# Two weight loads moved to ScalarE's queue, and two small gate operations moved from VectorE to GpSimd, in a kernel of attention and two feed-forward layers

## The chip, the cores and the metric

The kernel runs on one core of one Trainium2 chip. The metric is the time of one execution on the device in microseconds, as the median of several runs. The engines are TensorE (PE in the profile, its weight loads PEld), VectorE (DVE), ScalarE (ACT), GpSimd (POOL) and SyncE (SP), which here only issues transfers.

## The reference

Attention over 4 batches, 8 heads, 576 positions and 64 features per head, mixed with a read from a memory matrix M, then two feed-forward layers over 2304 tokens of width 512 with an inner width of 2048. All inputs are float32.

```python
a = softmax(causal(q @ k.T / sqrt(D)))            # row sums + 1e-9 in the denominator
local = a @ v
q_p = where(q > 0, q, exp(q) - 1) + 1             # phi
mem_out = (q_p @ M_prev) / (q_p @ z_prev + 1e-6)
g = 1 / (1 + exp(-beta))                          # one number per head
x = g * mem_out + (1 - g) * local                 # -> (2304, 512)
h = x @ w_in;  x = (s * relu(h)**2 + b) @ w_out   # layer 1
h = x @ w_in2; out = (h * tanh(softplus(h))) @ w_out2   # layer 2
```

The weights arrive with 64 bits a number; the kernel converts them to float32 itself.

## The kernel before

**Attention.** A unit is one head of one batch. Its query tiles of 128 rows come in two groups, TA (tiles 0 to 2) and TB (tiles 3 and 4). For batch 0 the two groups are units of their own: first TA of all eight heads, then TB of all eight; these 16 units are called early and multiply in plain float32 with 64 rows. The other 24 units (batches 1 to 3) take both groups. In a unit, phi of the query rows is made by GpSimd (line 500), ScalarE (501) and VectorE (502); VectorE multiplies by z and sums (494, 495), which gives the norm in the tile `nm`. The norm gets its epsilon and the head's gate `igate[:, 0, h]` at line 498, in `norm_gate`, and VectorE's reciprocal at line 506. GpSimd then scales phi by it into the first 64 columns of P's rows (557). The scores' maximum is taken by VectorE (545), the exponential and its row sums `rs` by ScalarE (554). The sums get their epsilon and gate `igate[:, 1, h]` at line 574, in `norm`, and a reciprocal at 576; P's rows are multiplied by the result on GpSimd, VectorE or ScalarE (569, 571), by tile. TensorE transposes P (598), multiplies with M and v (626), and the result goes through `xs` (634) to `x_d` in device memory (640).

**Weights.** Each of the 32 pieces of layer 1 (128 rows, 512 numbers of 64 bits) is loaded by SyncE (693) into a `raw` buffer and converted by ScalarE (700, 705, 717) and VectorE (707, 709, 711, 720). The first two raw buffers are the two first thirds of the tile `stage`; four more lie in tiles of later weights.

**Layers.** Layer 1 (products at lines 803 and 877) takes blocks of 256 tokens, later 512. It loads x from `x_d` (820) once all heads of the block's rows are stored, and runs interleaved with the later units. Layer 2 (1009, 1075) follows.

**Order.** Every step is given to a planner with an engine, an expected duration in microseconds, a priority, and the buffers it reads and writes. `Plan.order` simulates the engines and takes on each free engine the ready step with the lowest priority number; the order in which steps start there is the program order on each engine, and each engine works strictly in that order. A change of a duration or of an engine therefore gives another order of the whole program. `NONE` is a pseudo engine for steps that issue nothing. The planner also fills TensorE's planned idle time between 7 and 165 us with products of zeros (`zero_product`, line 1245).

Of the kernel before, what the change touches and what calls it, by code (L numbers as in the profile page):

```python
# [9 lines left out]
F32 = mybir.dt.float32  # L10
F32R = mybir.dt.float32r
BF16 = mybir.dt.bfloat16
I32 = mybir.dt.int32
# [3 lines left out]
ALU = mybir.AluOpType  # L17
AXIS = mybir.AxisListType.X
PSUM = bass.MemoryType.PSUM
DRAM = bass.MemoryType.DRAM  # L20

P = 128
MASKED = -1.0e30
HUGE = 3.0e38
PE, ACT, DVE, POOL, DMA = range(5)
# [25 lines left out]
def act_us(n, extra=0):  # L51
    return 0.094 + 0.00083 * n + 0.093 * extra


def dve_us(n, fast=False):
    return 0.068 + (0.00052 if fast else 0.00104) * n


def pool_us(n):
    return 0.38 + 0.0028 * n  # L60
# [6 lines left out]
def on(letter):  # L67
    return {"A": ACT, "D": DVE, "P": POOL}[letter]
# [111 lines left out]
class Plan:  # L180
# [29 lines left out]
    def add(self, engine, us, prio, f, r=(), w=(), after=(), keep=(), share=1.0):  # L210


        bufs = list({id(b): b for b in (*r, *w, *keep) if b.ring is not None}.values())
        new = [b for b in bufs if b.maker is None]
        waits = {id(s): s for b in r for s in b.writers}
        waits.update((id(s), s) for s in after)
        s = Step(engine, us, prio, f, list(waits.values()), bufs, new)
        s.share = share
        s.left = len(waits)
        for x in waits.values():  # L220
            x.next.append(s)
        for b in bufs:
            b.users += 1
            if b.maker is None:
                b.maker = s
            elif id(b.maker) not in waits:
                b.maker.next_start.append(s)
                s.left += 1
        for b in w:
            b.writers.append(s)  # L230
        self.steps.append(s)
        return s
# [100 lines left out]
def attention_then_two_ffn(ctx: ExitStack, tc: tile.TileContext, qk, qz, vm, beta,  # L333
# [3 lines left out]
    nc = tc.nc  # L337
# [22 lines left out]
    NONE = 5  # L360
    plan = Plan()
    add = plan.add
# [12 lines left out]
    igate = const.tile([P, 2, H], F32, name="igate")  # L375
# [9 lines left out]
    y_in = {j: Buf() for j in range(NT // N1)}  # L385
    wi_in, wo_in, wi_split = ({} for _ in range(3))

    nc.scalar.dma_start(igate[:, 1], beta.partition_broadcast(P))
    nc.scalar.preload_act_table_set("natural_log_exp_and_others")
    nc.scalar.dma_start(sb[:, 0:1], s1.partition_broadcast(P))  # L390
    nc.scalar.dma_start(sb[:, 1:2], b1.partition_broadcast(P))
# [4 lines left out]
    nc.vector.tensor_scalar_add(igate, igate, 1.0)  # L396
    nc.scalar.copy(zeros, mask[:, :P])

    psum = ctx.enter_context(tc.tile_pool(name="psum", bufs=1, space=PSUM))
    banks = [Bank(psum.tile([P, 512], F32, name=f"bank{i}")) for i in range(8)]  # L400
    stage = Home(ctx.enter_context(tc.tile_pool(name="stage", bufs=1, side="right")), "stage", 3072)
    m1 = ctx.enter_context(tc.tile_pool(name="m1", bufs=1))
    small, att = ExitStack(), ExitStack()
    m1s = small.enter_context(tc.tile_pool(name="m1s", bufs=1))
# [28 lines left out]
    def unit(b, h, prio, groups=(TA, TB), place=None):  # L433
# [4 lines left out]
        def add(engine, us, f, r=(), w=(), keep=(), share=1.0, lag=0.0):  # L438
            attention_steps.append(plan.add(engine, us, prio, f, r, w, keep=keep, share=share))
            attention_steps[-1].lag = lag  # L440
# [45 lines left out]
        nm = Buf(R["nm"], [P, 16])  # L486
        lo_t, n_t = tiles[0], len(tiles)
        mine = slice(lo_t, lo_t + n_t)
# [6 lines left out]
            nc.vector.tensor_reduce(nm.t[:, mine], q_rows(), axis=AXIS, op=ALU.add)  # L495

        def norm_gate():
            nc.vector.tensor_scalar(nm.t[:, mine], nm.t[:, mine], 1e-6, igate[:, 0, h:h + 1], op0=ALU.add, op1=ALU.mult)

        add(POOL, 0.4 + 0.0022 * n_t * D, lambda: nc.gpsimd.tensor_scalar_min(ex.t[:, mine], q_rows(), 0.0), [qn_b], [ex])  # L500
        add(ACT, act_us(n_t * D), lambda: nc.scalar.activation(ex.t[:, mine], ex.t[:, mine], AF.Exp), [ex], [ex])
        add(DVE, dve_us(n_t * D), lambda: nc.vector.scalar_tensor_tensor(ex.t[:, mine], q_rows(), 0.0, ex.t[:, mine],
                                                                         op0=ALU.max, op1=ALU.add), [ex, qn_b], [ex])
        add(DVE, 2 * dve_us(n_t * D), norm_phi, [ex, qn_b], [nm, qn_b])
        add(DVE, 0.13, norm_gate, [nm], [nm])
        add(DVE, 0.09, lambda: nc.vector.reciprocal(nm.t[:, mine], nm.t[:, mine]), [nm], [nm])  # L506


# [52 lines left out]
        def norm(tiles):  # L561

            def sums():
                return rs.t[:, tiles[0]:tiles[-1] + 1]

            def scale(t, e):
                x, r = Pt[t].t[:, D:P * (t + 1)], rs.t[:, t:t + 1]
                if e == ACT:
                    nc.scalar.activation(x, x, AF.Copy, scale=r)
                else:  # L570
                    (nc.vector if e == DVE else nc.gpsimd).tensor_scalar(x, x, r, None, op0=ALU.mult)  # L571

            gated, done = Buf(), Buf()
            add(DVE, 0.13, lambda: nc.vector.tensor_scalar(sums(), sums(), 1e-9, igate[:, 1, h:h + 1], op0=ALU.add, op1=ALU.mult),
                [rs_in[t] for t in tiles], [gated], [rs])
            add(DVE, 0.09, lambda: nc.vector.reciprocal(sums(), sums()), [gated], [done], [rs])  # L576
            for t in tiles:
                e = on((E_NORM if early else F_NORM)[t])
                n = D + P * t
                us = act_us(n, 1) if e == ACT else 0.08 + dve_us(n, True) if e == DVE else pool_us(n)  # L580
                add(e, us, lambda t=t, e=e: scale(t, e), [done, Pt[t]], [Pt[t]], [rs])
# [84 lines left out]
    def w_at(nm, r, j):  # L666
        return W[nm, r].t[:, j]
# [8 lines left out]
    def convert(layer, prio, which, r, j, raw, after=()):  # L676


        w_in, w_out = ((w_in1, w_out1), (w_in2, w_out2))[layer - 1]
        fc = r * FPR + j  # L680
        src = w_in[j * P:(j + 1) * P, r * 512:(r + 1) * 512] if which == "in" else w_out[fc * P:(fc + 1) * P, :]
        w = Buf(R["w32"], [P, 512], I32)

        def words():
            return raw.t[:, :1024].rearrange("p (n two) -> p n two", two=2)

        def limbs():
            return raw.t[:, :1024].bitcast(U16).rearrange("p (n four) -> p n four", four=4)

        def f32():  # L690
            return w.t.bitcast(F32)

        add(DMA, 1.5, prio, lambda: nc.sync.dma_start(words(), src.bitcast(I32).rearrange("p (n two) -> p n two", two=2)),
            w=[raw], after=after).lag = 1.4 if layer == 1 else 3.0

        e = on((C_W if layer == 1 else C2_W)[j])
        add(e, 0.567 if e == ACT else 0.335, prio,
            (lambda: nc.scalar.activation(f32(), words()[:, :, 1].bitcast(F32), AF.Copy, scale=2.0 ** -112)) if e == ACT else  # L700
            (lambda: nc.vector.tensor_scalar(f32(), words()[:, :, 1].bitcast(F32), 2.0 ** -112, None, op0=ALU.mult)),
            [raw], [w])

        low_words = Buf()
        add(ACT, 0.567, prio, lambda: nc.scalar.activation(words()[:, :, 0], words()[:, :, 0].bitcast(U32), AF.Copy,
                                                          scale=2.0 ** -29), [raw], [low_words])
        add(DVE, 0.335, prio, lambda: nc.vector.tensor_scalar(w.t, w.t, 3, None, op0=ALU.logical_shift_left), [w], [w])
        signed = Buf()
        add(DVE, 0.542, prio, lambda: nc.vector.tensor_scalar(limbs()[:, :, 1], limbs()[:, :, 3], 0x8000, None, op0=ALU.bitwise_and),
            [raw, low_words], [signed])  # L710
        add(DVE, 0.605, prio, lambda: nc.vector.tensor_tensor(w.t, w.t, words()[:, :, 0], op=ALU.add), [raw, signed, w], [w])  # L711
        if layer == 1:
            hi, lo = f"w{which[0]}h", f"w{which[0]}l"
            hi_dve, lo_dve = C_HI[j] == "D", C_LO[j] == "D"
            half = Buf()
            add(DVE if hi_dve else ACT, 0.335 if hi_dve else 0.52, prio,
                lambda: (nc.vector.tensor_copy if hi_dve else nc.scalar.copy)(w_at(hi, r, j), f32()), [w],
                [W[hi, r], half])
            add(DVE if lo_dve else POOL, 0.6 if lo_dve else 1.23, prio,
                lambda: (nc.vector if lo_dve else nc.gpsimd).tensor_tensor(w_at(lo, r, j), f32(),  # L720
                                                                           w_at(hi, r, j).bitcast(F32), op=ALU.subtract),
                [w, half], [W[lo, r]])
        return w
# [18 lines left out]
    def sums(prio, out, table):  # L742
        for f in table:
            def one(f=f):
                o_, x, y, op = f()
                nc.vector.tensor_tensor(o_, x, y, op=op)

            add(DVE, dve_us(256), prio, one, out[1:], out[:1])
# [383 lines left out]
    for h in range(H):  # L1132
        unit(0, h, PRE_A + STEP_A * h, (TA,), PLACE_A[h % 4])
    for h in range(H):
        unit(0, h, PRE_B + STEP_B * h, (TB,), PLACE_B[h])
# [21 lines left out]
    for i in range(len(seq) + LAG1):  # L1157
        if i < len(seq):
            j, fc = seq[i]
# [4 lines left out]
            n = len(plan.steps)  # L1164
# [4 lines left out]
        if i >= LAG1:  # L1169
            j, fc = seq[i - LAG1]  # L1170
            n = len(plan.steps)
# [3 lines left out]
            if fc == NFC - 1:  # L1175
                n = len(plan.steps)
# [17 lines left out]
    n = len(plan.steps)  # L1194
# [25 lines left out]
    n = len(plan.steps)  # L1220
# [72 lines left out]
```

## Time and profile before

| | |
|---|---|
| median of 3 runs | 1020.19 us (1019.63 to 1021.12) |
| time of the profiled execution | 1016.28 us |
| its span | 1014.3 us |
| TensorE busy | 997.1 us, 98% |
| VectorE busy | 840.7 us, 83% |
| ScalarE busy | 716.1 us, 71% |
| GpSimd busy | 207.8 us, 20% |

The span runs from the first to the last instruction of one profiled execution; its own time includes what lies around it. TensorE's busy time includes the zero products. A busy share is a mean over stages that differ.

### The profile page before, as it was taken

The page shows a single profiled execution, that of the slowest core. Times are in us where ns is not written, and L with a number is a line of the kernel's source. Part 1 is how long each engine was busy: PE and PEld are TensorE (multiplying, and loading weights), DVE is VectorE, ACT ScalarE, POOL GpSimd, SP SyncE. Part 2 cuts the span into 40 slices and gives each one's busy share as a digit, 9 for nine tenths or more (in the row PEclk, how much of TensorE's full clock was granted, in tenths as well). Part 3 has the DMA queues.
Part 4 walks back from the last instruction along what each step waited for, and adds up shares of the span by engine and source line. Part 5 has one row for each costly group of instructions (what it writes and reads, how often), then busy time and mean ns, then how long its engine had stood idle before and what let it go on. Part 6 is the DMA issues. An engine that isn't in the chain of part 4 may idle for free.

```text
span 1014.3 us, 19945 instructions
## 1 busy us (share of the span) xinstructions
PE 997.1 (98%) x6754; PEld 927.5 (91%) x6754; DVE 840.7 (83%) x2163; ACT 716.1 (71%) x1606; POOL 207.8 (20%) x330
## 2 busy tenths in 40 slices
PE   6999999999999999999999999999999999999998
PEld 4658799999999999999888888899999999999998
DVE  7989999999999999986788885279975789567864
ACT  6988798788888788876879997456653466434552
POOL 7841133334344334320000000000010000000010
PEclk9999999999999999999999999999999999999999
DMA  9764553324423433307889986468687665766464
GB/s 272 209 176 143 163 178 99 112 83 122 129 83 101 119 94 99 102 21 216 265 273 311 300 288 216 146 224 270 208 299 258 217 221 176 262 223 219 145 224 171
DMA packets 88981, 188.60 MB, mean 186 GB/s; under 512 B 8752, under 2 KB 63024, under 8 KB 81584
## 3 DMA queue, kind: packets, MB, share of 16 engines
q1 hardware_dynamic: 81392, 135.95, 43.1%
q0 software_dynamic: 7056, 51.38, 15.0%
q8 instruction: 53, 0.87, 0.3%
q14 instruction: 48, 0.39, 0.1%
q10 hardware_dynamic: 432, 0.01, 0.0%
HBM read 144.32 MB, written 42.99 MB: 185 GB/s over the span
## 4 chain that ended last, share of the span: by engine, by line
PE 69%; issue 18%; DVE 6%; POOL 3%; DMA 3%; ACT 1%; SPq 0%; POOLq 0%; DVEq 0%; ACTq 0%
PE bank L877 19%; PE bank L803 19%; PE bank L1009 9%; PE bank L1075 6%; PE bank L626 6%; PE bank L598 4%; PE bank L540 2%; PE bank L541 2%; PE bank L536 1%; POOL Pt L571 1%; DMA woh<-wi_split_d 1%; DVE stage L711 1%; DVE Pt L545 1%; POOL wol L990 1%; DMA stage<-in_w_in 1%
## 5 line engine op out<-in xcount | busy, mean ns | idle before, releaser
L1075 PE MATMUL bank<-woh,S 128*128 128x256 f32 x792 | 107.2, 283 | 0.0
L1075 PEld LDWEIGHTS bank<-woh,S 128*128 128x128 f32 x792 | 100.8, 192 | 0.0
L1075 PE MATMUL bank<-wol,S 128*128 128x256 f32 x720 | 98.1, 283 | 0.0
L557 POOL TENSOR_SCALAR Pt<-ex,nm 128x64 f32<-128x64 f32 x148 | 73.5, 513 | 112.8 <-DVE nm L506 48.9
L1009 PE MATMUL bank<-wi,woh 128*128 128x384 f32 x426 | 94.1, 335 | 0.1
L1075 PEld LDWEIGHTS bank<-wol,S 128*128 128x128 f32 x720 | 91.8, 192 | 0.0
L554 ACT ACTIVATE Pt<-Pt,mx 128x64 f32<-128x64 f32 (+4 forms) x148 | 81.6, 553 | 12.2 <-DVE mx L545 11.9
L990 POOL DMA_DIRECT2D wol<-wo_split_d x17 | 9.2, 540 | 353.6 <-DVE wi L732 261.8
L1009 PEld LDWEIGHTS bank<-wi,woh 128*128 128x128 f32 x426 | 75.6, 188 | 0.8 <-DMA woh<-wi_split_d 0.3
L1009 PE MATMUL bank<-wi,wol 128*128 128x384 f32 x294 | 76.1, 334 | 0.0
L598 PE MATMUL bank<-ident,Pt 128*128 128x128 f32 x432 | 65.6, 278 | 3.8 <-POOL Pt L571 3.6
L571 POOL TENSOR_SCALAR Pt<-Pt,rs 128x64 f32<-128x64 f32 (+2 forms) x68 | 54.4, 832 | 61.1 <-DVE rs L576 47.9
L606 DVE TENSOR_TENSOR PTl<-bank,PTh 128x128 fp32r<-128x128 f32 (+1 forms) x144 | 64.2, 481 | 1.4 <-ACT PTh L603 0.8
L545 DVE CUSTOM_DVE_ANT_0 Pt<-bank,mask 128x320 f32<-128x320 f32 (+3 forms) x148 | 59.7, 416 | 2.0 <-PE bank L541 1.0
L598 PEld LDWEIGHTS bank<-ident,Pt 128*128 128x128 f32 x432 | 49.1, 141 | 10.7 <-POOL Pt L571 7.5
L603 ACT CAST PTh<-bank 128x128 fp32r<-128x128 f32 (+1 forms) x144 | 55.3, 432 | 2.4 <-PE bank L598 1.2
L877 PE MATMUL bank<-gl,woh 128*128 128x256 f32 x320 | 53.7, 290 | 0.0
L877 PE MATMUL bank<-gh,wol 128*128 128x256 f32 x320 | 53.3, 289 | 0.0
L1009 PEld LDWEIGHTS bank<-wi,wol 128*128 128x128 f32 x294 | 53.0, 188 | 0.2
L877 PE MATMUL bank<-gh,woh 128*128 128x256 f32 x320 | 52.2, 285 | 0.0
L803 PE MATMUL bank<-xh,wi 128*128 128x256 f32 x320 | 51.4, 287 | 0.6 <-DVE rt L854 0.4
L848 ACT ACTIVATE rt<-bank,sb 128x256 f32<-128x256 f32 x80 | 38.0, 475 | 17.6 <-PE bank L803 16.1
(280 smaller groups left out, 2900.7 us busy)
## 6 DMA issues: line engine op xcount, KB each, us to landing
wol<-wo_split_d POOLq DMA_DIRECT2D x17, 1024.0 KB, 5.3
woh<-wo_split_d POOLq DMA_DIRECT2D x16, 1024.0 KB, 5.4
qk<-in_qk SPq DMA_DIRECT2D x24, 608.0 KB, 3.9
stage<-in_w_out SPq DMA_DIRECT2D x23, 512.0 KB, 4.2
wo_split_d<-high SPq DMA_DIRECT2D x44, 256.0 KB, 3.8
stage<-in_w_in SPq DMA_DIRECT2D x21, 512.0 KB, 5.0
stage<-wi_d SPq DMA_DIRECT2D x24, 384.0 KB, 4.6
wi_split_d<-woh SPq DMA_DIRECT2D x8, 1024.0 KB, 4.8
```

Source lines behind the costliest of these rows:

```text
L545: nc.vector.tensor_tensor_reduce(Pt[t].t[:, D + lo:D + hi], ps.t[:, :hi - lo], mask[:, SP - w + lo:SP - w + hi], -SCALE, mx.t[:, t:t + 1] ...
L554: nc.scalar.activation(Pt[t].t[:, D:w + D], Pt[t].t[:, D:w + D], AF.Exp, bias=mx.t[:, t + i:t + i + 1], scale=-1.0, accum_out=rs.t[:, t:t ...
L557: add(POOL, 0.48, lambda: nc.gpsimd.tensor_scalar(Pt[t].t[:, :D], ex.t[:, t, :], nm.t[:, t:t + 1], 1.0, op0=ALU.mult, op1=ALU.mult), [ex, ...
L571: (nc.vector if e == DVE else nc.gpsimd).tensor_scalar(x, x, r, None, op0=ALU.mult)
L598: nc.tensor.transpose(ps.t[:, c - c0, :], Pt[t].t[:, c * P:(c + 1) * P], ident)
L603: (nc.vector.tensor_copy if dve else nc.scalar.copy)(PT[0].t[:, at_], ps.t[:, :n])
L606: nc.vector.tensor_tensor(PT[1].t[:, at_], ps.t[:, :n], PT[0].t[:, at_].bitcast(F32), op=ALU.subtract)
L626: nc.tensor.matmul(o.rearrange("p (t q) -> p t q", q=P), v, x.t[:, f[0]:f[-1] + 1:f[1] - f[0] if len(f) > 1 else 1, :], start=(c == 0 and ...
L803: nc.tensor.matmul(ph, w_at(nm, r, cc)[:, o:o + P], x_at(x, cc), start=(part == 0 and cc == 0), stop=(part == 2 and cc == NCC - 1))
L877: nc.tensor.matmul(acc[ec // per].t[:, (ec % per) * n:(ec % per + 1) * n], w_at(nm, r, jj)[:, ec * P:(ec + 1) * P], t(x), start=(big and f ...
L1009: nc.tensor.matmul(ps.t[:, :H2], w[i // 4].t[:, j, kk, i % 4], x[kk].t[:, k], start=begin and part == kk == 0, stop=part == 2 and kk == 1, ...
L1075: nc.tensor.matmul(acc[t].t[:, :DH], s.t[:, j, t * P:(t + 1) * P], x.t[:, k, q % 4], start=q == part == 0, stop=q == NQ2 - 1 and part == 2)
```

## The change

The two parts of the change are independent in the code. The loads of the first two pieces of w_in are issued from ScalarE's queue right behind the load of beta, before the plan; in the plan they are steps of the pseudo engine that are said to be ready after 5.5 and a further 1.0 us. The PSUM pool, the banks and the stage tile are made earlier in the code for that. And lines 498 and 574 are issued on GpSimd, with a planned duration of 0.39 us in place of 0.13.

```diff
@@ -385,7 +385,14 @@
+    psum = ctx.enter_context(tc.tile_pool(name="psum", bufs=1, space=PSUM))
+    banks = [Bank(psum.tile([P, 512], F32, name=f"bank{i}")) for i in range(8)]
+    stage = Home(ctx.enter_context(tc.tile_pool(name="stage", bufs=1, side="right")), "stage", 3072)
+
     nc.scalar.dma_start(igate[:, 1], beta.partition_broadcast(P))
+    for j in range(2):
+        nc.scalar.dma_start(stage.tile([P, 1024], I32, 1024 * j, "raw").rearrange("p (n two) -> p n two", two=2),
+                            w_in1[j * P:(j + 1) * P, :512].bitcast(I32).rearrange("p (n two) -> p n two", two=2))
     nc.scalar.preload_act_table_set("natural_log_exp_and_others")
...
-    psum = ctx.enter_context(tc.tile_pool(name="psum", bufs=1, space=PSUM))
-    banks = [Bank(psum.tile([P, 512], F32, name=f"bank{i}")) for i in range(8)]
-    stage = Home(ctx.enter_context(tc.tile_pool(name="stage", bufs=1, side="right")), "stage", 3072)
@@ -495,14 +499,14 @@
         def norm_gate():
-            nc.vector.tensor_scalar(nm.t[:, mine], nm.t[:, mine], 1e-6, igate[:, 0, h:h + 1], op0=ALU.add, op1=ALU.mult)
+            nc.gpsimd.tensor_scalar(nm.t[:, mine], nm.t[:, mine], 1e-6, igate[:, 0, h:h + 1], op0=ALU.add, op1=ALU.mult)
...
-        add(DVE, 0.13, norm_gate, [nm], [nm])
+        add(POOL, 0.39, norm_gate, [nm], [nm])
@@ -571,7 +575,7 @@
-            add(DVE, 0.13, lambda: nc.vector.tensor_scalar(sums(), sums(), 1e-9, igate[:, 1, h:h + 1], op0=ALU.add, op1=ALU.mult),
+            add(POOL, 0.39, lambda: nc.gpsimd.tensor_scalar(sums(), sums(), 1e-9, igate[:, 1, h:h + 1], op0=ALU.add, op1=ALU.mult),
                 [rs_in[t] for t in tiles], [gated], [rs])
@@ -690,8 +694,11 @@
-        add(DMA, 1.5, prio, lambda: nc.sync.dma_start(words(), src.bitcast(I32).rearrange("p (n two) -> p n two", two=2)),
-            w=[raw], after=after).lag = 1.4 if layer == 1 else 3.0
+        if layer == 1 and which == "in" and r == 0 and j < 2:
+            add(NONE, (5.5, 1.0)[j], prio, lambda: None, w=[raw])
+        else:
+            add(DMA, 1.5, prio, lambda: nc.sync.dma_start(words(), src.bitcast(I32).rearrange("p (n two) -> p n two", two=2)),
+                w=[raw], after=after).lag = 1.4 if layer == 1 else 3.0
```

## Rows read from the trace of the kernel before

**Rows 1.** Busy time by stage: us; PE, PEld, DVE, ACT, POOL busy (instructions); clock; DMA share; GB/s.

```profile
0.00:74.01 74.01, 62.61 (x309) 41.81 (x309) 62.89 (x205) 59.76 (x162) 52.16 (x73) 1.00 0.77 223
74.01:140.00 65.99, 65.99 (x435) 54.60 (x436) 61.91 (x184) 56.58 (x129) 12.79 (x23) 1.00 0.51 154
140.00:170.00 30.00, 28.48 (x229) 27.23 (x228) 29.76 (x80) 24.71 (x59) 10.03 (x13) 1.00 0.41 128
170.00:460.00 290.00, 289.21 (x2334) 283.90 (x2334) 274.18 (x882) 240.99 (x641) 106.69 (x174) 1.00 0.33 96
460.00:1014.30 554.30, 550.75 (x3454) 519.97 (x3453) 411.99 (x816) 334.07 (x619) 26.09 (x49) 1.00 0.71 235
```

**Rows 2.** The same for line 1245, the zero products (PE and PEld busy).

```profile
0.00:74.01 74.01, 21.52 (x119) 17.17 (x119) 1.00 0.77 223
74.01:140.00 65.99, 1.19 (x6) 0.81 (x6) 1.00 0.51 154
140.00:170.00 30.00, 6.30 (x36) 5.12 (x36) 1.00 0.41 128
```

**Rows 3.** Chain of waits up to 170 us: start, us, what.

```profile
2.51 5.44 DMA stage<-in_w_in
56.58 1.04 POOL Pt L571
66.56 5.40 DMA xr<-x_d
74.29 0.47 PE bank L803 x4
```

**Rows 4.** Busy time by stage again, the stretch of the eight heads.

```profile
8.71:60.65 51.94, 47.45 (x245) 32.54 (x244) 48.91 (x161) 46.09 (x130) 47.93 (x59) 1.00 0.83 244
```

**Rows 5.** Timeline, ScalarE and VectorE at the first piece: start, duration, engine; idle before.

```profile
7.97 0.66 ACT L700 ACTIVATE stage<-stage 128x512 f32<-128x512 f32 x1 [2.80 <-DMA stage<-in_w_in]
...
8.67 0.43 DVE L707 TENSOR_SCALAR stage<-stage 128x512 int32<-128x512 int32 x1 [1.99 <-ACT stage L700]
```

**Rows 6.** VectorE's time by stage in line 498 (first three) and 574.

```profile
8.71:60.65 51.94, 2.77 (x8) 1.00 0.83 244
60.65:170.00 109.35, 2.22 (x10) 1.00 0.49 150
170.00:460.00 290.00, 5.28 (x21) 1.00 0.33 96
...
8.71:60.65 51.94, 1.82 (x8) 1.00 0.83 244
60.65:170.00 109.35, 2.90 (x12) 1.00 0.49 150
170.00:460.00 290.00, 10.14 (x44) 1.00 0.33 96
```

**Rows 7.** GpSimd's groups by form, 3.7 to 60.65 us: busy us, mean ns.

```profile
L557 POOL TENSOR_SCALAR Pt<-ex,nm 128x64 f32<-128x64 f32 x22 | 14.0, 657 | 1.4 <-DVE nm L506 0.7 <-DVE mx L545 0.6
L500 POOL TENSOR_SCALAR ex<-qn 128x128 f32<-128x128 f32 x1 | 1.6, 1551 | 0.0
L500 POOL TENSOR_SCALAR ex<-qn 128x192 f32<-128x192 f32 x2 | 1.4, 692 | 0.2
L500 POOL TENSOR_SCALAR ex<-wih 128x128 f32<-128x128 f32 x1 | 0.5, 527 | 0.0
```

**Rows 8.** Line 557 alone, 7 to 64 us: shortest, median, longest ns.

```profile
L557 POOL TENSOR_SCALAR Pt<-ex,nm x22: 309/422/2508, 10.2 to 60.3; 128x64 f32<-128x64 f32 x22
```

**Rows 9.** Timeline of VectorE around a gate.

```profile
66.80 0.22 DVE L574 TENSOR_SCALAR rs<-rs,igate 128x2 f32<-128x2 f32 x1
66.93 0.74 DVE L709 TENSOR_SCALAR wih<-wih 128x512 uint16<-128x512 uint16 x1
```

**Rows 10.** A conversion instruction of VectorE, 8.71 to 60.65 us: busy us, mean ns.

```profile
L709 DVE TENSOR_SCALAR stage<-stage 128x512 uint16<-128x512 uint16 x6 | 4.6, 763 | 0.0
```

**Rows 11.** GpSimd's waits, 170 to 460 us: total us, times, longest.

```profile
POOL ex L500 <- DMA qn<-in_qz: 33.6, 13, 4.1
```

## The prediction

> **What bounds the kernel now.** I read the profile by stages first: the span cut where the work changes, with the busy time of each engine in each piece [rows 1], and beside it how much of TensorE's time in those pieces is its filler, the products of a tile of zeros that keep it occupied and compute nothing [rows 2]. The reader is to see that TensorE does nothing useful for 74.01 - 62.61 + 21.52 = 32.9 us before layer 1 starts at 74, for 1.2 us from 74 to 140, for 30.00 - 28.48 + 6.30 = 7.8 us from 140 to 170, for 0.8 us from 170 to 460, and for 3.6 us after that. That is 46.3 us out of 1014.3, and everything else is products that the change leaves alone. So the end can move only by the moment at which layer 1 begins, and by the 9.0 us lost between 74 and 170. All pieces show the granted clock at 1.00, so the clock has no part in it.
>
> Then the chain that ended last, up to 170 us [rows 3]. Layer 1's first product at 74.29 waits for the load of x at 66.56 (5.40 us), which waits for the last of the eight heads of the first unit group; that head was released by a multiplication on GpSimd at line 571. The chain starts with a weight piece whose load takes 5.44 us from 2.51. In the stretch in which the eight heads run, from 8.71 to 60.65, no engine has room: VectorE is busy 48.91 us of 51.94, GpSimd 47.93, ScalarE 46.09 [rows 4]. From 140 to 170 VectorE is busy 29.76 of 30.00 while TensorE wastes its 7.8 us: there VectorE sets the pace [rows 1, 2].
>
> **The change part by part.**
>
> *The first two pieces from ScalarE's queue.* ScalarE waits 2.80 us for the first piece and starts on it at 7.97; behind it VectorE idles 1.99 us [rows 5]. Its load is the fourth that SyncE issues, at 2.51. ScalarE's queue can issue it right behind the load of beta, about 1.3 us earlier, and with the same 5.44 us it lands 1.3 us earlier. That is the gain's end: -1.3 us. The other end: the two pieces are 1 MB, the chip moved 244 GB/s in the stretch that follows [rows 4], so they take 4.3 us, and q and k of the first head, issued by SyncE meanwhile, could land up to 4.3 us later. SyncE loses two issues and so issues the other heads' loads a little earlier; ScalarE issues two more before its table load, in a time when it has nothing else. I take -0.5 us: a short idle stretch on VectorE is partly filled, and part of it is given back by the first head's loads.
>
> [...] The rows show one queue's loads landing some 5 us after their issue, and nothing of two queues side by side. [...]
>
> *Gates on GpSimd, first stage.* 16 gates lie between 8.71 and 60.65 (8 at line 498, 8 at line 574), 22 between there and 170, and 65 from 170 to 460 [rows 6]. GpSimd has no instruction of 2 to 5 elements a row. The nearest is line 557, 64 elements with the same two scalar operands: 309 ns at its shortest, 422 in the median, 657 as the mean of 22 in this stretch [rows 7, 8]. Below it the price is bounded by line 500: 527 ns at 128 elements and 692 at 192 [rows 7] make 2.6 ns an element and leave 0.20 us for none. So a gate costs between 0.20 and 0.66 us, 3.2 to 10.5 us for 16. I take 0.40, nearest to the median with fewer elements: 6.4 us. Against it stand GpSimd's idle 4.0 us in the stretch [rows 4], of which I count half, and 2.1 us of later units' work at line 500 (128 elements, 527 and 1551 ns) [rows 7] that can move behind the heads: +2.3 us on layer 1's start. The bounds: if all 4.0 us are usable nothing is left on GpSimd, and VectorE's relief, 2.1 us below, brings the heads forward, -2.1; if no idle time is usable and each gate costs 0.66, it is 10.5 - 2.1 = +8.4. Each gate also adds two hand-overs (VectorE or ScalarE to GpSimd, GpSimd to VectorE) to each head's chain; two heads are in flight, so I put them within these bounds. Behind a gate on GpSimd stand lines 557 and 571, for which the transposes on TensorE wait; behind the reciprocal on VectorE stand conversions and the next head's scores.
>
> *VectorE's relief.* The gates' own time is 4.6 us before 60.65 and 5.1 us from there to 170 [rows 6], but VectorE overlaps small instructions: a gate starts at 66.80 and the next instruction at 66.93 [rows 9]. What leaves VectorE is thus nearer 0.13 us a gate: 2.1 us in the first stretch, which goes to conversions that have to be done by 170 anyway, and 2.9 us after it, 5.0 in sum. Between 74 and 170 TensorE wastes 9.0 us and VectorE is the bound where most of it is lost, so I take -4.0 us; the bounds are 0 (nothing reaches TensorE) and -9.0 (all of the waste, with the gates at their full time).
>
> *From 170 to 460.* TensorE wastes 0.8 us there [rows 1]; the 65 gates can give back at most that: -0.5 us, cover being TensorE itself, which is full. VectorE has 290.00 - 274.18 = 15.8 us to spare, and 65 x 0.13 = 8.5 more. If that cover were gone, each wait of VectorE for GpSimd would count in full; that is the third rival.
>
> **Sum.** -0.5 + 2.3 - 4.0 - 0.5 = -2.7 us. The profiled execution's span is 1014.3 us and its own time 1016.28; by the sum they become 1011.6 and 1013.6. The median before is 1020.19, 3.9 above the profiled execution, so the time I give is 1020.2 - 2.7 = 1017.5.
>
> **The rivals.**
>
> *GpSimd becomes the pace of the heads (slower).* For it: GpSimd is busy 92% of the first stage, and one and the same instruction takes 309 to 2508 ns there [rows 8], so it is held by something. Against it: 4.0 us idle and work that can move. With gates at 0.66 us and no idle time used, layer 1 starts 8.4 us later; with -4.0 and -0.5 given back and nothing from the pieces the sum is +3.9: 1024.1. It decides as soon as layer 1's start moves by over 5 us, that is, from 16 x c - 4.1 = 5, a gate at 0.57 us. If each gate has to sit out one whole conversion instruction of VectorE, 763 ns in the mean of line 709 [rows 10], on top of 309 ns, it costs 1.07 us; layer 1 then starts 16 x 1.07 - 4.1 = 13 us later, and the time is 13 - 4.5 = 8.5 above, 1028.7. The spread of line 557 allows it; its median of 422 ns speaks against every gate paying it. [...]
>
> *The two sides cancel (no change).* The start moves by +2.3 and VectorE's relief is spent on waits for the gates, so that only 2 us of the 9.0 come back: 1020.2 within a microsecond. For it: each relieved VectorE instruction is replaced by a wait for another engine. Against it: the order on each engine is planned anew, with the gate's own cost, so other work is put between.
>
> *VectorE waits behind GpSimd in the long stage (slower).* From 170 on GpSimd stands idle at line 500 for q, 33.6 us over 13 waits [rows 11]. A gate that is queued behind such a wait holds the reciprocal, and VectorE with it. VectorE's room is 15.8 + 8.5 = 24.3 us, 0.37 us for each of 65 gates; at 0.5 us each the loss is 8 us: 1028. Against it: line 502 on VectorE already depends on GpSimd and ScalarE, and GpSimd is only 37% busy there.
>
> **How the numbers follow.** This measurement tells a change from none at about 0.2%, 2 us. Forecast (faster, 1011 to 1018): 0.47. Cancelling, within 2 us either way: 0.26. GpSimd the pace: 0.18; every gate behind a whole VectorE instruction: 0.03. Waits in the long stage: 0.04; first head's loads late by most of 4.3 us: 0.02. So faster 0.47, same 0.26, slower 0.27. The forecast's own range is 1012 to 1018.1; to leave out no more than 2 in 10 the range goes from 1011 (the pieces at -1.3, the start unmoved, -8 of the waste) to 1025 (the first rival and a little).
>
> **What would show it.** Right: the first conversion on ScalarE starts near 6.7 us instead of 7.97; gates on GpSimd last 0.2 to 0.66 us; layer 1's first product lies at 74 to 78; the zero products after 140 shrink from 6.30 us to under 3. Wrong: layer 1 starts after 79; GpSimd is busy over 97% up to then and lines 557 and 571 follow each other without a gap; VectorE shows idle time at the two reciprocals; the first scores on TensorE start after the first piece's conversion. The sum would also be wrong if the new order alone, with no price behind it, puts a conversion before a head's work: then the start moves with GpSimd not full.

## The result and the profile after

The changed kernel takes 1026.95 us (median of 7 runs, 1022.64 to 1030.21) against 1019.63 us for the kernel before on the same chip (7 runs): ratio 1.0066, 95% interval 1.0045 to 1.0086. It is slower; the forecast was 1017.5 and its range ended at 1025. The profiled execution has a span of 1021.1 us and a time of 1022.83.

Busy time by stage of the changed kernel (columns as in [rows 1]; the last window runs past the end of the span at 1021.1), and then the zero products, now at line 1252 (as in [rows 2]):

```profile
0.00:74.01 74.01, 56.51 (x260) 38.12 (x260) 56.76 (x168) 53.36 (x143) 57.04 (x87) 1.00 0.71 201
74.01:140.00 65.99, 64.92 (x408) 51.03 (x408) 57.47 (x164) 55.44 (x127) 17.74 (x38) 1.00 0.53 161
140.00:170.00 30.00, 29.48 (x227) 27.66 (x226) 29.46 (x81) 26.72 (x68) 10.97 (x18) 1.00 0.53 159
170.00:460.00 290.00, 288.97 (x2354) 285.58 (x2355) 270.92 (x831) 243.86 (x651) 132.05 (x244) 1.00 0.33 97
460.00:1100.00 640.00, 555.61 (x3490) 524.53 (x3488) 413.70 (x820) 335.82 (x622) 26.09 (x49) 1.00 0.62 203
```

```profile
0.00:74.01 74.01, 22.02 (x112) 17.32 (x112) 1.00 0.71 201
74.01:140.00 65.99, 2.17 (x14) 1.79 (x14) 1.00 0.53 161
140.00:170.00 30.00, 0.96 (x4) 0.68 (x4) 1.00 0.53 159
170.00:460.00 290.00, 1.53 (x9) 1.20 (x9) 1.00 0.33 97
```

The time without useful products before 74 grows from 32.9 to 74.01 - 56.51 + 22.02 = 39.5 us. From 74 to 140 it grows from 1.2 to 3.2, and from 140 to 170 it falls from 7.8 to 30.00 - 29.48 + 0.96 = 1.5. After that it grows again, from 0.8 to 290.00 - 288.97 + 1.53 = 2.6 up to 460 and from 3.6 to 1021.10 - 460.00 - 555.61 = 5.5 from there to the end. In sum TensorE loses 6.0 us more, of the 6.8 by which the span grows. VectorE does 6.1 us less work in the first stage and 3.3 less from 170 to 460 [rows 1]; GpSimd does 4.9 and 25.4 more. So the loss is at the start, most of it comes back by 170, and 3.7 us are lost after 170. In the timeline layer 1's first product moves from 74.13 us to

```profile
87.55 1.70 PE L810 MATMUL bank<-xh,wi 128*128 128x256 f32 x12
```

which is 13.4 us, while the span grows by 6.8. I read that as follows: conversions and later units that stand between layer 1's first products in the kernel before are done by then in the changed one. The window from 140 to 170 agrees (7.8 to 1.5 us); no run tests it alone.

In the timeline of SyncE the first and the eighth head's result go to device memory at these times, first in the kernel before and then in the changed one (start, duration):

```profile
20.64 0.50 SPq L640 DMA_DIRECT2D x_d<-xs  x1
...
65.33 0.55 SPq L640 DMA_DIRECT2D x_d<-xs  x1
```

```profile
29.51 0.55 SPq L644 DMA_DIRECT2D x_d<-xs  x1
...
76.77 0.55 SPq L644 DMA_DIRECT2D x_d<-xs  x1
```

The first head is 8.9 us late already, the eighth 11.4. Two things have to be explained: what happens before 29 us, and what keeps the heads from making it up.

The first half stands in ScalarE's timeline. The kernel before made the gate's exponential and then the first head's at

```profile
4.50 0.22 ACT L395 ACTIVATE igate<-igate 128x16 f32<-128x16 f32 x1 [2.05 <-DVE igate L394]
...
4.81 0.36 ACT L501 ACTIVATE ex<-ex 128x192 f32<-128x192 f32 x1
```

and the changed kernel at

```profile
1.17 0.94 ACTq L394 DMA_DIRECT2D stage<-in_w_in  x2
2.14 1.28 ACT L396 ACT_TABLE_LOAD   x1 [2.14 <-issue]
8.48 0.33 ACTq L397 DMA_DIRECT2D sb<-in_s  x1
9.72 0.33 ACTq L398 DMA_DIRECT2D sb<-in_b  x1
10.11 0.21 ACT L402 ACTIVATE igate<-igate 128x16 f32<-128x16 f32 x1 [6.68 <-DMA wih<-in_vm]
...
10.41 0.66 ACT L707 ACTIVATE stage<-stage 128x512 f32<-128x512 f32 x1
...
10.97 0.35 ACT L505 ACTIVATE ex<-ex 128x192 f32<-128x192 f32 x1
```

The reader is to see the hole between 3.42 and 8.48. The pieces are issued at 1.17 as forecast. The first piece is there when it was forecast: it lands 5.6 us after its issue, near 6.8. But the loads of s and b (512 bytes each), which stood right behind beta, now stand behind the pieces, and each waits: s is issued when the first head's q and k have landed (8.48), b when its v has (9.72), and SyncE issued both of these. Four loads of SyncE wait in the same way: two that start at 6.75 and 9.40 for the two pieces (1.5 and 2.1 us), two that start at 10.34 and 11.76 for loads of the second head (0.6 and 1.1). The trace shows these waits; what ties each load to the one it waits for was not shown. All of ScalarE's arithmetic stands behind the two loads of 512 bytes in the program, and the first of it starts at 10.11, where the kernel before had it at 4.50.

The first head's loads also land later beside the pieces. Loads by group, first 6.5 us (KB, median us to landing), first of the kernel before and then of the changed one:

```profile
wih<-in_qk SPq DMA_DIRECT2D x1, 192.0 KB, 5.1
...
wih<-in_vm SPq DMA_DIRECT2D x1, 96.0 KB, 4.8
```

```profile
wih<-in_qk SPq DMA_DIRECT2D x1, 192.0 KB, 7.3
...
wih<-in_vm SPq DMA_DIRECT2D x1, 96.0 KB, 7.8
```

The gates themselves cost what was expected. Shortest, median and longest ns of the two lines on GpSimd, whole span:

```profile
L502 POOL TENSOR_SCALAR nm<-nm,igate x40: 268/277/889, 12.8 to 427.1; 128x5 f32<-128x5 f32 x24, 128x3 f32<-128x3 f32 x8, 128x2 f32<-128x2 f32 x8
L578 POOL TENSOR_SCALAR rs<-rs,igate x64: 266/271/1423, 16.9 to 448.8; 128x3 f32<-128x3 f32 x32, 128x2 f32<-128x2 f32 x32
```

### The profile page after: what moved, and what is told of

Same layout as the page of the kernel before. It is cut to its first block, busy times and chain, and to the rows that moved or that the text cites. A ratio compares the mean times of both kernels' runs of the same rounds, so it can differ in the third digit from the quotient of the medians.

```text
span 1021.1 us, 19790 instructions
## 1 busy us (share of the span) xinstructions
PE 995.5 (97%) x6733; PEld 926.9 (91%) x6733; DVE 828.3 (81%) x2059; ACT 715.2 (70%) x1606; POOL 243.9 (24%) x434
## 4 chain that ended last, share of the span: by engine, by line
PE 68%; issue 17%; DVE 4%; DMA 4%; POOL 3%; ACT 2%; SPq 0%; POOLq 0%; ACTq 0%
PE bank L884 18%; PE bank L810 18%; PE bank L1016 9%; PE bank L1082 6%; PE bank L630 6%; PE bank L602 4%; PE bank L540 2%; PE bank L544 2%; PE bank L545 2%; DMA xr<-x_d 1%; DMA woh<-wo_split_d 1%; POOL Pt L575 1%; DMA woh<-wi_split_d 1%; DMA wol<-in_qz 1%; POOL wol L997 1%
## 5 line engine op out<-in xcount | busy, mean ns | idle before, releaser
L561 POOL TENSOR_SCALAR Pt<-ex,nm 128x64 f32<-128x64 f32 x148 | 65.8, 459 | 30.0 <-PE bank L602 16.4
L578 POOL TENSOR_SCALAR rs<-rs,igate 128x3 f32<-128x3 f32 (+1 forms) x64 | 27.8, 435 | 93.4 <-ACT Pt L558 88.5
```

Of the source, the lines that this page charges most:

```text
L561: add(POOL, 0.48, lambda: nc.gpsimd.tensor_scalar(Pt[t].t[:, :D], ex.t[:, t, :], nm.t[:, t:t + 1], 1.0, op0=ALU.mult, op1=ALU.mult), [ex, ...
```

## The experiments

Theories: the queue (Q): the two small loads behind the pieces hold ScalarE. The landing (B): the first heads' loads land later beside the pieces, wherever the small loads stand. The order (O): the new plan, with durations that don't hold, puts other work ahead of the heads. GpSimd's room (F): the gates queue among its longer instructions in the heads' stretch. The hand-over (H): each gate costs VectorE a wait, wherever it stands. Each ratio is to the kernel before on the same chip. "Start" is layer 1's first product (before: 74.1). "New order" is a plan made anew for the edit; "old order" is the program order of before, the edit made in the issued instruction alone.

**Each part alone, and the small loads ahead of the pieces (new orders).** e1 has the loads without the gates, e2 the gates without the loads. e3 is the whole change and e4 the loads alone, both with this (an excerpt):

```diff
     nc.scalar.dma_start(igate[:, 1], beta.partition_broadcast(P))
+    nc.scalar.dma_start(sb[:, 0:1], s1.partition_broadcast(P))
+    nc.scalar.dma_start(sb[:, 1:2], b1.partition_broadcast(P))
     for j in range(2):
...
     nc.scalar.preload_act_table_set("natural_log_exp_and_others")
-    nc.scalar.dma_start(sb[:, 0:1], s1.partition_broadcast(P))
-    nc.scalar.dma_start(sb[:, 1:2], b1.partition_broadcast(P))
```

> Only the loads of the first two pieces are moved; both gates stay on VectorE. Theory Q (ScalarE's queue): the two 512-byte loads of s and b stand behind the pieces on ScalarE's queue, wait there for q/k and v of the first head to land, and hold the first exponential from 4.5 to about 10.1 us as in the changed kernel; layer 1's first product comes at 79 to 81 instead of 74 and the time is 3 to 6 us above the kernel before. Theory G (GpSimd's gates make the whole loss): the start of layer 1 within 1.5 us of 74, time within 2 us of the kernel before.

> Only the two gates are moved to GpSimd; the pieces are loaded by SyncE as before. Theory G: GpSimd is full in the first stage, layer 1's first product comes at 79 to 81, time 3 to 6 us above the kernel before. Theory Q alone: the start at 72 to 76, time within 2 us of the kernel before or a little below it.

> The whole change, with the loads of s and b issued ahead of the two pieces on ScalarE's queue. Theory Q: the first exponential on ScalarE starts by 6 us instead of 10.1, layer 1's first product comes 3 to 5 us earlier than in the changed kernel (87.6), at 82 to 85, time 1022 to 1025. Rival B (the pieces take the DMA engines from the first heads' loads, wherever the small loads stand): the first head's scores start at 8.5 us or later all the same, and the start of layer 1 stays within 1.5 us of 87.6, time 1026 to 1029.

> Only the loads moved, s and b ahead of the pieces, gates on VectorE. Theory Q: layer 1 starts at 74 to 76, time within 2 us of the kernel before. Rival B: layer 1 starts at 78 or later, time 3 us or more above it. By the prediction's own term the pieces in time give 0.5 us.

| | ratio (95%) | start |
|---|---|---|
| e1 | 1.0061 (1.0043 to 1.0079) | 84.0 |
| e2 | 1.0044 (1.0028 to 1.0060) | 87.0 |
| e3 | 1.0051 (1.0032 to 1.0069) | 87.8 |
| e4 | 1.0088 (1.0063 to 1.0113) | 91.9 |

Either part alone makes the kernel slower, and its start lies later than either expectation has it, so neither is innocent. With the small loads first the hole is gone: the gate's exponential lies at 5.36 in e3. Yet the time hardly moves. ScalarE's timeline of e3 shows what stands there instead:

```profile
8.65 0.66 ACT L707 ACTIVATE stage<-stage 128x512 f32<-128x512 f32 x1 [2.88 <-DMA stage<-in_w_in]
9.21 0.35 ACT L505 ACTIVATE ex<-ex 128x192 f32<-128x192 f32 x1
```

The plan thinks the first piece is there at 5.5 and puts its conversion ahead of the first head's exponential; ScalarE waits for the piece until 8.65, and the head with it. That is the order (O), and e4 holds it too. In e1 and in the changed kernel the conversion also stands ahead, but there both come late (10.41 and 10.97), so it costs the head only 0.56 us.

**The order taken apart.** e5 keeps the plan of the gates on GpSimd and issues them on VectorE; e6 keeps the old order and issues them on GpSimd; e8 is e4 with the plan told when the pieces land; e7 gives GpSimd the gates of batches 1 to 3 only, with loads as before and a new plan.

```diff
 e6, both gate lines: nc.vector.tensor_scalar -> nc.gpsimd.tensor_scalar, add(DVE, 0.13, ...) unchanged
 e5: add(DVE, 0.13, ...) -> add(POOL, 0.39, ...), nc.vector unchanged
 e8: -            add(NONE, (5.5, 1.0)[j], prio, lambda: None, w=[raw])
     +            add(NONE, (8.6, 2.9)[j], prio, lambda: None, w=[raw])
 e7: (nc.vector if early else nc.gpsimd), add(DVE if early else POOL, 0.13 if early else 0.39, ...)
```

> The planner is told that the gates run on GpSimd for 0.39 us, so the order of the program is that of the run with the gates alone moved, but the two instructions are issued on VectorE. Theory O (the new order is what costs): layer 1's first product comes at 83 to 88 as in that run (87.0), and the time is 3 to 6 us above the kernel before. Theory G (GpSimd's gates, as work and as waits): the start falls back to 74 to 79 and the time to within 2 us of the kernel before.

> The order of the kernel before, with the two gates issued on GpSimd at their old places. Theory G: GpSimd is pushed back by 16 gates of 0.27 to 0.9 us, layer 1 starts at 80 or later, time 3 us or more above the kernel before. Theory O: layer 1 starts at 74 to 78 and the time is within 2 us of the kernel before.

> Gates on GpSimd only in the 24 units of batches 1 to 3; the 16 early units and the loads as before. Theories G and O agree that the start of layer 1 stays at 74 to 75. If VectorE's relief is worth what the prediction says, the 0.8 us after 170 and part of the 7.8 us before it come back: 0.5 to 2 us below the kernel before. Third rival of the prediction (VectorE waits behind GpSimd in the long stage): 3 us or more above it.

> Only the loads moved, s and b ahead of the pieces, and the planner is told that the pieces are there at 8.6 and 11.5 us, as the chip showed, in place of 5.5 and 6.5. Theory P (wrong due times put the first conversion ahead of the first head's exponential): that exponential starts by 6 us instead of 9.3, layer 1 starts 4 us or more earlier than in the same kernel with the old times (91.9), time within 3 us of the kernel before. Theory O (any new order costs): layer 1 starts at 83 or later and the time is 3 us or more above the kernel before.

e5: 1.0115 (1.0097 to 1.0133). It decides nothing: VectorE does the gates in an order made for GpSimd, and its start is not known.

e8: 1.0068 (1.0051 to 1.0084), start 82.8. With the true landing times the first head's exponential starts at 5.69 us, and the start lies 9.1 us before that of e4; the intervals of the two ratios overlap. But e10 below, the same loads in the old order, has 1.0010 and a start of 75.8, so 0.6% comes with the new order even here. ScalarE's timeline of e8 shows the fault of e3 again, one piece later:

```profile
12.18 0.19 ACT L558 ACTIVATION_READ_ACCUMULATOR Pt<-Pt,mx 128x1 f32 x1
15.71 0.68 ACT L712 ACTIVATE wih<-wih 128x512 int32<-128x512 uint32 x1 [3.35 <-DMA wih<-in_w_in]
16.29 0.55 ACT L558 ACTIVATE Pt<-Pt,mx 128x320 f32<-128x320 f32 x1
```

A conversion of the third piece, which SyncE loads, now stands ahead of the first head's next exponential (line 558, which was 554) and waits 3.35 us for its load. The first head's result goes out at 26.39 us, 3.3 later than in e10.

e6: 1.0069 (1.0057 to 1.0081), start 83.2: the gates cost no less with no new order at all. VectorE's waits of e6 from 3 to 90 us (total us, times, longest):

```profile
DVE rs L576 <- POOL rs L574: 4.3, 6, 1.2
DVE nm L506 <- POOL nm L498: 3.3, 5, 1.3
```

e7: 0.9974 (0.9959 to 0.9990), 1016.81 us, start 74.4; it is faster than the kernel before. Its stages after 140, and the zero products from 140 to 170:

```profile
140.00:170.00 30.00, 27.99 (x224) 26.65 (x223) 29.77 (x78) 25.44 (x64) 13.66 (x21) 1.00 0.44 129
170.00:460.00 290.00, 288.33 (x2339) 283.75 (x2339) 265.93 (x816) 242.16 (x641) 115.84 (x236) 1.00 0.34 99
```

```profile
140.00:170.00 30.00, 3.34 (x20) 2.71 (x20) 1.00 0.44 129
```

VectorE is relieved by 8.3 us from 170 to 460 [rows 1], and TensorE loses 30.00 - 27.99 + 3.34 = 5.4 us from 140 to 170, where it lost 7.8. The mechanism of the prediction's -4.0 is there, smaller.

**The loads in the old order, and GpSimd with room.** e9 has the loads from ScalarE's queue and the gates on VectorE, with the plan as if SyncE issued the loads; e10 is e9 with s and b first. e11 is e6 and e12 the kernel before, both with GpSimd's multiplications of P by `rs` cut to 16 columns in the early units (the other columns stay unscaled), so that GpSimd has room.

```diff
 e9: -            add(NONE, (5.5, 1.0)[j], prio, lambda: None, w=[raw])
     +            add(DMA, 1.5, prio, lambda: None, w=[raw], after=after).lag = 1.4
 e11, e12, in scale: +   x = x[:, :16] if early and e == POOL else x
```

> The two pieces are loaded from ScalarE's queue as in the change, but the planner still counts them as SyncE's loads, so the order on the compute engines is that of the kernel before; gates on VectorE. Theory Q (the two small loads hold ScalarE's queue): first exponential near 10 us, the first head's store of x 4 to 6 us later than the 20.6 of before, the pace of the other heads unchanged (44.7 us from the first to the eighth store), layer 1 starts at 78 to 81, time 2 to 5 us above the kernel before. Theory O (the new order costs, not the queue): layer 1 starts at 74 to 76, time within 2 us.

> The same with the loads of s and b ahead of the pieces on ScalarE's queue. Theory Q: the first exponential by 6 us, first store of x at 21 to 23, layer 1 starts at 74 to 76, time within 2 us of the kernel before. Rival B (the pieces take the DMA engines from the first heads' loads): first store at 24 or later, layer 1 at 77 or later, time 2 us or more above it.

> The old order with both gates on GpSimd, and GpSimd's multiplications of P in the 16 early units cut to the first 16 columns of each row (the rest stays unscaled): some 15 us less work for GpSimd before layer 1. Theory F (GpSimd is full): layer 1 starts within 1.5 us of the next run, which has the same cut with gates on VectorE. Theory H (each gate is two hand-overs, and engines that work in a fixed order wait at both): layer 1 starts 4 us or more later than in the next run, with VectorE waiting at the two reciprocals for 4 us or more in sum.

> The kernel before with the same cut of GpSimd's multiplications in the early units (the rest of those rows stays unscaled), gates on VectorE. If GpSimd's work sets the pace of the eight heads, layer 1 starts at 68 or earlier instead of 74; if VectorE and ScalarE set it as much, at 71 to 74.

e9: 1.0031 (1.0019 to 1.0042), start 79.1, first head's result at 26.23, 5.6 us late. e10: 1.0010 (1.0000 to 1.0021), start 75.8, first result at 23.11. ScalarE's timeline of e10:

```profile
5.39 0.21 ACT L402 ACTIVATE igate<-igate 128x16 f32<-128x16 f32 x1
...
5.70 0.36 ACT L505 ACTIVATE ex<-ex 128x192 f32<-128x192 f32 x1
```

Both theories hold, with sizes: moving the small loads ahead (Q) gives back 3.1 of the first head's 5.6 us; 2.5 stay, with q and k landing 6.3 us after issue and not 5.1 (B). The first piece doesn't come earlier in e10 either: issued at 2.14 us behind the small loads, it is there at 8.81, against 7.97 before. And e1 against e9, the same loads in new and old order: 1.0061 against 1.0031, intervals apart. That is O again.

e12: 0.9997 (0.9982 to 1.0013), start 75.7. e11: 0.9990 (0.9975 to 1.0005), start 74.3. GpSimd's busy time in the stretch of the heads, fifth of the numbers with a count, in e6, e11 and e12:

```profile
8.71:60.65 51.94, 45.92 (x207) 31.93 (x207) 40.73 (x128) 39.52 (x108) 46.58 (x66) 0.95 0.74 224
```

```profile
8.71:60.65 51.94, 48.11 (x243) 33.46 (x243) 45.91 (x144) 45.95 (x130) 42.86 (x75) 1.00 0.80 242
```

```profile
8.71:60.65 51.94, 48.83 (x238) 34.63 (x237) 46.33 (x158) 44.11 (x127) 30.98 (x57) 1.00 0.80 238
```

With its other work cut, GpSimd makes the same gates at no cost to the start, and VectorE's waits for them are 2.5 and 0.5 us, not 4.3 and 3.3. So the hand-over as such (H) is not the price; GpSimd's room (F) is. And e12 shows that GpSimd was not the pace before: with 17 us less of its work the start comes no earlier (75.7, later than either expectation). It was just short of setting the pace.

**Both parts in the old order, and the gates by stage.** e13 is e9 and e6 together. e14 is e6 with only the heads' first group in batch 0 (TA, the heads that layer 1's start waits for) on GpSimd, e15 with all but it.

```diff
 e14, both gate lines: nc.vector -> (nc.gpsimd if first_half else nc.vector)
 e15, both gate lines: nc.vector -> (nc.vector if first_half else nc.gpsimd)
```

> Both parts of the change as they are issued, in the order of the kernel before. If the two delays of the start add up (79.1 with the loads alone and 83.2 with the gates alone, against 74.3), layer 1's first product lies at 88 and the time is some 9 to 10 us above that of the kernel before, ratio 1.009 to 1.010; the whole change (87.55, ratio 1.0066) then gains 2 to 3 us by its new order. If they lie beside each other, since heads that begin later find GpSimd with more idle time, the start is at 83 to 85 and the ratio 1.006 to 1.007, and the new order moves the start later but not the end.

> Old order, loads as before, gates on GpSimd only in the first group of the eight heads of batch 0. If GpSimd's lack of room in that stretch is the whole price, layer 1's first product lies at 83, as with all gates on GpSimd, and the ratio is 1.006 to 1.008. If waits of VectorE for the gates all along the program make the price, the ratio is 1.001 to 1.002 and the start at 76 at most.

> Old order, loads as before, gates on GpSimd everywhere but in the first group of the eight heads. If the price lies in that stretch alone, layer 1's first product stays at 74 to 75 and the ratio is 0.997 to 1.000: the gain of VectorE's relief with no new plan behind it. If later waits for the gates cost as much, the ratio is 1.004 or above with the start unmoved.

e13: 1.0092 (1.0078 to 1.0107), start 86.2. In time the parts add up, 0.31% + 0.69% against 0.92%; the start comes 1.9 us short of the sum of the two delays. Its first head's result goes out at 26.59 us, 6.0 late, so of the 8.9 us in the changed kernel 2.9 come with the new order; that part was not traced. e14: 1.0087 (1.0066 to 1.0108), start 83.1: 16 gates make all of the 0.69%. e15: 0.9991 (0.9980 to 1.0002), start not known. TensorE's waits in e14 (start, duration; idle before) and then its stages around them:

```profile
52.56 0.33 PE L598 MATMUL bank<-ident,Pt 128*128 128x128 f32 x1 [0.21 <-POOL Pt L571]
...
53.80 0.44 PE L598 MATMUL bank<-ident,Pt 128*128 128x128 f32 x2 [0.67 <-POOL Pt L571]
...
55.85 0.90 PE L598 MATMUL bank<-ident,B 128*128 128x128 f32 x3 [1.27 <-POOL B L571]
```

```profile
53.00:54.00 1.00, 0.33 (x5) 0.21 (x3) 0.19 (x1) 0.74 (x2) 0.90 (x2) 1.00 1.00 298
54.00:55.00 1.00, 0.59 (x5) 0.38 (x3) 0.78 (x2) 0.73 (x2) 0.91 (x2) 1.00 1.02 276
55.00:56.00 1.00, 0.15 (x1) 0.15 (x2) 0.00 (x0) 0.72 (x2) 0.90 (x2) 0.71 1.06 277
56.00:62.00 6.00, 6.00 (x18) 3.46 (x19) 4.72 (x12) 1.36 (x4) 5.91 (x9) 0.50 0.39 137
```

Here the delay grows. TensorE waits for line 571 on GpSimd, is busy 1.07 us of three, and then shows a granted clock of 0.50 for six, in which it is busy throughout. The fifth head's result is 5.4 us late in e14, the sixth, on the other side of that stretch, 9.6.

**How much of it is clock.** e16 is the changed kernel once more. e17 is the changed kernel and e18 is e14, each with the zero products that the plan puts between 30 and 80 us issued twice:

```diff
             s.f()
+            if self.fill and s.f is self.fill[3] and 30.0 < s.start < 80.0:
+                s.f()
```

> The changed kernel once more, beside the next two on one chip. If the loss of clock is part of the result, its runs again spread with the mean clock: near 1022.7 us at 1.00 and near 1029 at 0.992. If the clock has no part in it, runs with the same clock spread as much as runs with different ones.

> The changed kernel, but each product of zeros that the plan puts between 30 and 80 us is issued twice. If the lower clock makes the median 1027 and not 1022.7, and idle stretches of TensorE bring it about, the runs show a clock of 0.998 or more and the ratio is 1.003 to 1.004. If the start alone sets the time, the ratio stays at 1.006 to 1.007, or rises by the work added: at most some 10 us of zeros, where TensorE idles 17.5 us.

> Gates on GpSimd in the first eight heads alone, old order, with the zeros between 30 and 80 us issued twice. Without them the sixth head's store moved from 5.4 us late to 9.6 us late in a stretch at half clock. If the clock makes that step, it goes: layer 1 starts at 79 to 80 in place of 83.1, ratio 1.004 to 1.006 in place of 1.0087. If GpSimd alone makes it, start and ratio stay.

e16: 1.0082 (1.0056 to 1.0108). Of the 13 executions of the changed kernel in the two comparisons, five with a mean clock of 1.00 take 1023.6 us in the mean and six at 0.990 to 0.993 take 1029.6; one at 0.998 took 1025.17, one at 0.996 1028.08. e17: 1.0090 (1.0073 to 1.0106), start 91.6, clocks 0.998 to 1.00. e18: 1.0107 (1.0088 to 1.0125), start 85.0, clocks 0.998 to 1.00. The clock of that stretch comes back (1.00 from 50 to 60 us in e18, 0.77 in e14) and the step from the fifth head to the sixth shrinks from 9.9 to 6.8 us (5.7 before), but the time is no shorter: the zeros stand in the heads' way and, by the medians, cost as much as they save or more. Both expectations of a gain fall. That the lower clock goes with longer runs is shown; how much the median would gain from the clock alone isn't, since nothing here changed the clock alone.

## Why the prediction was wrong

**What bounds the kernel: right in the main.** The end moved with layer 1's start and with what came back between 74 and 170. I took each us of start for a us of time; here 13.4 us of start became 6.8 of span. And a late start also costs after 170, where I saw next to nothing to lose: 3.7 us more here. In e14, which has no gate on GpSimd after the heads, TensorE loses 5.5 us from 170 to 460 in place of 0.8. What causes this loss was not traced.

**The pieces, -0.5: wrong in sign.** The step that failed is "ScalarE issues two more before its table load, in a time when it has nothing else". It had the loads of s and b to issue behind them, and these wait for the first head's landings. In the old order the term is +3.2 us (e9); with the small loads ahead +1.0 (e10, interval 0.0 to 2.1), which is the late landing (q and k 6.3 us after their issue), within the bounds given. The first conversion was to start near 6.7 us, and its piece was there, but it started at 10.41. The other end of the term, q and k up to 4.3 us late, was an estimate; beside the pieces they landed after 7.3 us where they took 5.1, 2.2 later.

**Gates in the first stage, +2.3: the mechanism right, the size wrong.** A gate costs 0.47 us at line 502 (3.78 us for 8) and 0.41 at line 578 (2.47 for 6) in the heads' stretch, close to the 0.40 taken. What failed is counting half of GpSimd's idle 4.0 us as usable and the rest at its bare duration. The measured term is +9.0 us of start (e6, e14), just over the bound of +8.4, and +8.9 us of time in e14: gates queue behind instructions of up to 1.6 us (line 571 on 128 x 320: 1.59 in e14), line 571 waits behind gates, TensorE waits for line 571 (1.27 us at 55.85 in e14), and in some stretches the clock falls (to 0.50 in e14). Between the fifth and the sixth head, across such a stretch, e14 loses 4.2 of its 9.0 us. The rival "GpSimd becomes the pace" named this engine and place, but its point of decision, 0.57 us a gate, was not reached, and the start moved all the same. Its 1024.1 lies near the runs at full clock by luck: it takes nothing for the pieces and -4.5 for VectorE's relief, where the runs show +3.2 and at most -2.7. GpSimd was busy 60.08 us of the 78.84 from 8.71 to the start in the changed kernel, 76%, so the sign of 97% would have misled as well.

The other form of that rival, every gate behind a whole instruction of VectorE at 1.07 us, falls: medians of 271 and 277 ns. The longest gate took 1423 ns; what held it was not shown.

**VectorE's relief, -4.0, and the long stage, -0.5: real, too large.** Without the 16 gates of the first heads it is -0.9 us in the old order (e15, an interval that just includes no change), and -2.7 with a plan of its own and no gate of batch 0 moved (e7). From 170 to 460 VectorE waits for a gate once, 0.2 us, so the rival of waits in the long stage did not come.

**The clock, put at nothing.** "So the clock has no part in it" was read from the kernel before, where every piece shows 1.00. The changed kernel's runs at 1.00 take 1023.6 us in the mean, inside the stated range; the median of 1026.95 lies among those at 0.991 to 0.993. How much of the loss the clock makes by itself stays open (e17).

**The sum by the runs:** +3.2 (e9) + 8.9 (e14) - 0.9 (e15) = 11.2 us in the old order, and e13 measures 9.4. The whole change has 7 to 8 (1.0066 and 1.0082). The new order, named last among what would make the sum wrong, does put a conversion ahead of the first head. With the loads alone it costs 0.3% (e1 against e9; the conversion makes 0.56 us of its 4.9 us of start, the rest was not traced), and 0.6 to 0.8% with the small loads first (e8 and e4 against e10), where ScalarE is seen to wait for a piece ahead of the head (3.35 us in e8). It seems to give 0.25% back with the gates alone (e2 against e6, intervals that just touch). What it does in the whole change stays open: the intervals of 1.0066, 1.0082 and 1.0092 overlap.

## What to carry to other kernels

Before moving a load to a compute engine's queue, look at what that engine issues behind it: here two loads of 512 bytes waited there until 8.48 and 9.72 us for loads that SyncE had issued to land, and the engine's arithmetic waited with them, until 10.11. Small work moved to a lightly used engine is priced in the stage where it lands, by that engine's room there and by who waits behind it: gates of the same kind gave up to 2.7 us where GpSimd had room and took 8.9 where it had 8% idle. Due times written into a planner by hand decide the order around them, and a start that looks earlier on paper can put a wait in front of the first useful work (2.88 us in e3).

## What the runs showed of the hardware

- In the changed kernel a load of 512 bytes held ScalarE's queue from 3.42 to 8.48 us, until a load that SyncE had issued had landed.
- In the same profile, beside two loads of 512 KB from ScalarE's queue, a load of 192 KB that SyncE issued took 7.3 us to land and one of 96 KB 7.8; where the first of the two was issued behind them, by SyncE at 2.51 us, they took 5.1 and 4.8 (the kernel before).
- A gate on GpSimd, on 128 x 2 to 128 x 5 elements, took 266 ns at the shortest and 271 to 277 in the median, less than line 557 on 64 elements (309 at its shortest) [rows 8]; the longest took 1423.
- Three us in which TensorE was busy 1.07 were followed by six at a granted clock of 0.50 (e14). In the profile of the changed kernel it had no product at all from 63 to 64 us, and the clock stayed at 1.00 there; the same kernel's runs have mean clocks from 0.990 to 1.00.
